# Two normalised tiles turned by DMA instead of TensorE, all residual statistics on VectorE, and one attention split a slot later, in a one-core transformer block

## Chip, cores and metric

The kernel runs on one core of a Trainium2 chip. The metric is device time in microseconds of one execution of the whole program. A core has five engines with a queue each, all in order: TensorE (PE in the profile; PEld is its weight load), VectorE (DVE), ScalarE (ACT), GpSimd (POOL) and SyncE (SP), which here issues nearly all DMAs. An instruction waits on semaphores, and everything queued behind it on its engine waits with it.

## What is computed

One block on 2048 rows of 512 values: layer norm, attention with 32 heads of 16 in which each row sees itself and 7 earlier rows at distance 2, a product with `wo` and a residual sum; then layer norm, a product with `w1` (512 x 1792), squared ReLU, a product with `w2`, and a second residual sum.

```python
h  = x + attention(layernorm(x) @ wqkv) @ wo      # 8 keys per row, 2 apart, softmax
r  = max(layernorm(h) @ w1 + b1, 0)
h2 = h + (r * r) @ w2 + b2
```

All is in float32. The kernel splits each operand of a product in a high and a low part and sums three products of parts (high x high, low x high, high x low), so a product of a 128-row tile costs 12 matmuls of 128 x 512.

## The kernel before

The 2048 rows are 16 tiles t of 128. A first phase makes q, k and v of all tiles; then come four MLP stages, u = 0 to 3, each for the four tiles 4u to 4u + 3 together. While stage u runs its MLP, the attention and the `wo` product of the four tiles of stage u + 1 are done beside it. So tiles 4 to 7 are prepared in stage 0, 8 to 11 in stage 1, 12 to 15 in stage 2; i = t mod 4 is a tile's place in its stage (R = 4, RI = 2).

A stage is a loop over slots p = 0 to 16. Slot p gives TensorE, in this order, a `wo` product if one is due, the first MLP product of hidden block p (`mlp1`, up to p = 13) and the second of block p - 3 (`mlp2`), 12 matmuls each. The order of the instructions of all other engines is the order in which the program writes them, and that is planned by hand: functions are put in lists for a slot, and `end_slot` runs them: first `due` (put there by `at`), then `pump`, then `amid` (by `midway`), then `late` (by `after`). A function that is put in the list being run goes to that list's end.

`pump` draws steps of the attention of the next tiles from a generator. It keeps two clocks in estimated microseconds, `now["pe"]` and `now["dve"]`, and writes steps as long as `dve` is behind `pe`; when `dve` has come to within HALF = 2.6 of `pe` it first runs `amid`. Products add to `pe` (2.73 each), a tile's transposes add 0.44, `norm_stats` adds 0.93 to `dve`, the h add 0.7, `lo_T` of an attention tile 0.69, an attention step 0.26 to 1.55 times a factor of 1.05 to 1.08. The products that weigh the values (L351, VectorE) are summed by three adds on GpSimd (`add_up`, L408), which `pump` writes one step later; the last add writes a head group's part of `o`. An attention unit s serves the two tiles 2s and 2s + 1, in eight head groups.

The way of tile t in slots, with the lists of constants that set them: `load_h` (LH), the split of `o` in two 16-bit planes on ScalarE (`o_split`, L621), a transposing DMA on SP's queue (`turn_dma`, L625), the join of the planes on ScalarE (`o_join`, by `turn_join`, L630) with the casts to high and low part (tiles in OV; OP sets the slots), the `wo` product (WP), `h_add` on VectorE (L666), the statistics of h, the normalisation `h_norm` on ScalarE (L196), `add_b2` on GpSimd (L679) and `spill` of h to DRAM by SP (L682). The normalised tile `hn` must be turned too: for tiles in HV by split, DMA and join (`h_split`, `turn_dma`, `turn_join`, then the casts in `h_parts`), for the others by four transposes on TensorE into a PSUM bank (`h_T`, L201) with the casts read from there. For tiles with i = 2 and 3 of stages 0 and 1 `h_T` stands in slot 16, the last of the stage: the first ahead of the last `mlp2`, the second in its middle. The first product of the next stage reads the casts of all four tiles.

The statistics are made in two ways. Tiles in AS use `act_stats`: two long activations on ScalarE with a short one between (L182 to L184), written in `late`. The others use `norm_stats`: `bn_stats` and `bn_aggr` on VectorE (L163, L164). Either way three small GpSimd instructions, `finish` (L169 to L172, or L188 to L191), make the scale and the offset; `finish` is put in `late`.

SBUF tiles of the name "row" share ROWS = 15 buffers; the products and the transposes for the MLP stages take turns in two PSUM banks.

Of the kernel before, what the change touches and what calls it, by code (L numbers as in the profile page):

```python
# [19 lines left out]
R = 4  # L20
RI = 2
# [8 lines left out]
ROWS = 15  # L30
LAG = 3
HALF = 2.6
AS = (8, 9, 12, 13)
OV = tuple(range(4, 16))
HV = (0,1,4,5,8,9,12,13)
SLOW = 1.01, 1.08, 1.05
DELAY = 3
WJ = 2
# [8 lines left out]
WP = 9, 10, 13, 14  # L47
HP = 15, 15, 16, 16
# [10 lines left out]
def block_kernel(ctx, tc, x, wqkv, wo, w1, b1, w2, b2, out):  # L59
# [53 lines left out]
    def at(delta, fn, *a):  # L113
        due.setdefault(now["slot"] + delta, []).append((fn, a))

    def after(delta, fn, *a):
        late.setdefault(now["slot"] + delta, []).append((fn, a))
# [4 lines left out]
    def end_slot(pe):  # L122
        now["pe"] += pe
        run(due)
        pump()
        run(amid)
        run(late)
        now["slot"] += 1

    def run(chores):  # L130
        todo = chores.get(now["slot"], [])
        while todo:
            fn, a = todo.pop(0)
            fn(*a)

    def dve(t):
        now["dve"] += t
# [18 lines left out]

    stats = {}

    def norm_stats(key, src):
        st = small.tile([P, 6], F32, name="st")  # L160
        mv = small.tile([P, 2], F32, name="mv", bufs=4)
        rs = small.tile([P, 2], F32, name="rs", bufs=4)
        nc.vector.bn_stats(st, src)  # L163
        nc.vector.bn_aggr(mv, st)  # L164
        dve(0.93)
        stats[key] = mv, rs

        def finish():
            nc.gpsimd.tensor_scalar(out=rs[:, 1:2], in0=mv[:, 1:2], scalar1=EPS, scalar2=None,  # L169
                                    op0=ALU.add)  # L170
            nc.gpsimd.tensor_tensor(out=rs[:, 0:1], in0=rs[:, 1:2], in1=mhalf, op=ALU.pow)
            nc.gpsimd.tensor_scalar(out=rs[:, 1:2], in0=mv[:, 0:1], scalar1=rs[:, 0:1],  # L172
                                    scalar2=-1.0, op0=ALU.mult, op1=ALU.mult)
        after(0, finish)

    def act_stats(key, src):

# [263 lines left out]
    def x_stats(t):  # L441
        if t < XS:
            norm_stats(t, xt[t])
        else:
            act_stats(t, xt[t])
# [151 lines left out]
    def o_T(t):  # L597
        s, j = divmod(t, RI)
        pump(until=s)
        tr = transposes(o_t[s][:, j, :])  # L600
        if t % R == RI:

            ohl = att.tile([P, 2, KB, P], F32R, name="ohl", tag="o", bufs=3)
            oT[t] = ohl[:, 0], ohl[:, 1]
        else:
            oT[t] = row("oh", (P, KB, P), F32R), row("ol", (P, KB, P), F32R)
        at(0, hi_T, tr, [oT[t][0]])
        at(0, lo_T, tr, [oT[t][0]], [oT[t][1]])
# [55 lines left out]
    def h_add(t, ps):  # L664
        h = hs[t]
        nc.vector.tensor_tensor(out=h, in0=ps, in1=h, op=ALU.add)  # L666
        dve(0.7)
        if t in AS:
            after(0, act_stats, t, h)
        else:  # L670
            norm_stats(t, h)

    def h_norm(t):
        hn[t] = row("hn")
# [27 lines left out]
    def h_T(t):  # L702
        if t // R == R - 1:
            return last_h_T(t)
        tr = transposes(hn.pop(t), "mm")
        i = t % R
        hs_, ls_ = [a[:, :, i] for a in hh], [a[:, :, i] for a in hl]
        if len(turn["mm"].tags) > 2:
            at(0, hi_T, tr, hs_)
        else:  # L710
            due.setdefault(now["slot"], []).insert(0, (hi_T, (tr, hs_)))
        at(0, lo_T, tr, hs_, ls_)
# [169 lines left out]
    def mlp1(u, f):  # L882
        ps = turn["mm"].tile("mm")
        fs = slice(f * P, (f + 1) * P)
        mm3(ps, lambda k: w1_h[:, k, fs], lambda k: w1_l[:, k, fs],
            lambda k: hh[k // 2][:, k % 2], lambda k: hl[k // 2][:, k % 2])
        at(1, hidden, u, f, ps)
# [94 lines left out]
    for n in range(16):  # L982
        gp, t = divmod(n, 4)
# [28 lines left out]
    def first_phase(t0):  # L1012
        def chores(m):
# [16 lines left out]
            for t in range(R):  # L1030
                if k == OT[t]:
                    at(0, load_h, t)
                    o_T(t)
                if t in HV and k == HK[t][0]:
                    at(0, h_split, t)
                    after(0, turn_dma, ("h", t))
                if t in HV and k == HK[t][1]:
                    at(0, turn_join, ("h", t))
# [3 lines left out]
                if k == HT[t]:  # L1042
                    (at(0, h_parts, t) if t in HV else h_T(t))
            if k in W2:
# [11 lines left out]
    def load_w2(f):  # L1056
        raws[f] = row("raw2")
        nc.sync.dma_start(raws[f], w2[f * P:(f + 1) * P, :])
# [36 lines left out]
    for u in range(R - 1):  # L1095
        now["sub"] = u
        first, end = u == 0, False
        fs = list(range(FB)) if first else [*sorted(place), 12, 13]
        fs += [f for f in range(12) if f not in fs and (u < 2 or f not in ENDS)]
        fs += ENDS if u == 2 else []  # L1100
        need = [] if first else [f for f in fs if f < 12 and f not in place]
        acc = [psum.tile([P, D], F32, name="acc", tag=tag) for tag in ("acc0", "acc1", "tr0", "tr1")]
        js = range(R)


        todo, halves = {}, {}
        for i in js:
            t = R * (u + 1) + i
            if not end:
                a = i // 2 if u == 2 else 0  # L1110
                o0 = OP[i] - a - (2 if i >= RI and t in OV else 0)
                if t in OV:
                    turned = [(o0, after if i == RI else at, 0, o_split, t),
                              (o0, at if i > RI else after, i // (RI + 1), turn_dma, ("o", t)),
                              (o0 + 2, at, 0, o_join, t)]
                else:
                    turned = [(o0, o_T, t)]
                if t in HV:
                    h0 = 11 + i
                    turned += [(h0, midway, 0, h_split, t), (h0, after, 0, turn_dma, ("h", t)),  # L1120
                               (h0 + 2, at, 0, turn_join, ("h", t))]
                for p, *what in ((LH[i] - a, at, 0, load_h, t), *turned,
                                 (WP[i] - a, wo_product, t, (0, 1, 2 + 3 * a, 3 + 3 * a))):
                    todo.setdefault(p, []).append(what)
                p, h = (HP[i], i % 2) if u < 2 else HL[i]
                if t in HV:
                    todo.setdefault(p, []).append((at, 0, h_parts, t))
                else:
                    (todo, halves)[h].setdefault(p, []).append((h_T, t))
            todo.setdefault(UP[i], []).append((at, 0, unspill, R * u + i))  # L1130
        if u == 2:
            for p, *what in ((12, at, 0, t_load, 0), (12, at, 0, t_load, 1), (13, after, 0, t_sums, 0),
                             (13, after, 0, t_sums, 1), (13, at, 1, t_split, 0),
                             (14, after, 0, t_split, 1)):
                todo.setdefault(p, []).append(what)

        def half(p):
            run(due)
            for fn, *a in halves[p]:
                fn(*a)  # L1140

        for p in range(FB + LAG):
            more = 0.0
            if p == FB:
                run(due)
                dve(HOLD)
            if u < 2 and p == FB - 2:
                dve(HOLD)
            for fn, *a in sorted(todo.get(p, []), key=lambda x: x[0] is wo_product):
                fn(*a)  # L1150
                more += 2.73 if fn is wo_product else 0.0
            if p < FB:
                mlp1(u, fs[p])
                more += 2.73
                if first:
                    after(0, split_w2, p)
                    if p + 1 < FB:
                        load_w2(p + 1)
            q = p - LAG
            if q >= 0:  # L1160
                f = fs[q]
                mlp2(u, f, acc, js, q == 0, q == FB - 1,
                     (lambda: half(p)) if p in halves else None)
                more += 2.74
                if f < 12 and (need or first and p < FB - LAG):
                    free.append(place.pop(f))
                    if need:
                        at(1, fetch, need.pop(0))
            end_slot(more)
        for i in js:  # L1170
            at(u // 2, finish, R * u + i, acc[i])
# [48 lines left out]
    h = hs[S // P - 1]  # L1220
# [34 lines left out]
```

## Time and profile before

| what | us |
|---|---|
| median of 3 runs | 506.21 (505.8 to 506.57) |
| the profiled execution | 506.32 |
| its span, first to last instruction | 504.2 |
| TensorE busy | 497.7 (99%) |
| VectorE busy | 377.4 (75%) |
| GpSimd busy | 355.7 (71%) |
| ScalarE busy | 305.0 (60%) |

The granted TensorE clock is 1.000 over the span. In the trace stage 1 begins with the first product at 249.1 and stage 2 at 338.6. In the rows of the timeline the columns are start, length, engine, line, operation, out<-in, shapes, count, and in brackets the engine's idle time before the instruction with what ended it.

### The profile page before, as it was taken

What the parts mean: (1) busy time and instruction counts of PE and PEld (TensorE: products, weight loads), DVE (VectorE), ACT (ScalarE), POOL (GpSimd) and SP (SyncE); (2) the same over time, 40 slices, a digit from 0 to 9 for tenths busy, and PEclk for the clock granted to TensorE, in tenths of its full rate; (3) what the DMA queues carried; (4) which work ended last, traced back from release to release, by engine and by line L of the source; (5) the groups of instructions that cost most, each with busy time, mean ns of one, the idle gap of its engine ahead of it and who ended that gap; (6) DMA issues with size and microseconds to landing.
All of it is one profiled execution on the core that took longest, in us unless ns stands there. A gap on an engine that the chain in (4) does not pass through costs nothing.

```text
span 504.2 us, 7546 instructions
## 1 busy us (share of the span) xinstructions
PE 497.7 (99%) x2422; PEld 421.4 (84%) x2422; DVE 377.4 (75%) x512; ACT 305.0 (60%) x558; POOL 355.7 (71%) x434
## 2 busy tenths in 40 slices
PE   8999999999999999999999999999999999999997
PEld 7999888888888888888888888778888888998986
DVE  6379899988989899788879988998972047833233
ACT  4635777668346758378464657845566937666541
POOL 5614798886685999879677876896897464685610
PEclk9999999999999999999999999999999999999999
DMA  9668979989798898679577766767662372355212
GB/s 273 196 209 229 311 231 311 281 261 278 211 230 249 300 282 255 212 209 231 186 255 219 211 194 167 208 229 257 204 174 67 97 197 83 132 153 154 64 43 83
DMA packets 109359, 102.61 MB, mean 204 GB/s; under 512 B 29448, under 2 KB 77832, under 8 KB 109320
## 3 DMA queue, kind: packets, MB, share of 16 engines
q1 hardware_dynamic: 108376, 101.61, 68.4%
q10 hardware_dynamic: 944, 0.52, 0.3%
q8 instruction: 19, 0.31, 0.2%
q14 instruction: 20, 0.16, 0.1%
HBM read 72.65 MB, written 24.25 MB: 192 GB/s over the span
## 4 chain that ended last, share of the span: by engine, by line
PE 88%; ACT 4%; POOL 3%; DVE 2%; issue 1%; DMA 1%; POOLq 0%; ACTq 0%
PE mm L228 46%; PE acc L900 25%; PE wo L228 8%; PE mm L823 6%; PE tr L201 2%; POOL pr L408 1%; DMA xt<-in_A_x_dram 1%; ACT pl L621 1%; DVE pr L351 0%; ACT pl L630 0%; ACT big_l L152 0%; ACT r L877 0%; ACT r L876 0%; DVE s L759 0%; PE half L923 0%
## 5 line engine op out<-in xcount | busy, mean ns | idle before, releaser
L408 POOL TENSOR_TENSOR pr<-pr 128x512 f32<-128x512 f32 (+1 forms) x128 | 134.1, 1048 | 33.6 <-DVE pr L351 28.2
L228 PE MATMUL mm<-big_l,w_h 128*128 128x512 f32 x336 | 88.5, 389 | 0.1
L351 DVE TENSOR_TENSOR pr<-ex,v 128x1024 f32<-128x1024 f32 x64 | 78.0, 1220 | 12.2 <-POOL o L408 7.5
L340 DVE TENSOR_TENSOR pr<-qp,k 128x1024 f32<-128x1024 f32 x64 | 76.8, 1200 | 10.1 <-ACT qp L268 7.8
L374 DVE TENSOR_REDUCE ex<-pr 128x64 f32<-128x1024 f32 x64 | 78.5, 1226 | 1.9
L228 PEld LDWEIGHTS mm<-big_l,w_h 128*128 128x128 f32 x336 | 63.0, 188 | 13.6 <-ACT qp L268 0.5
L155 POOL TENSOR_TENSOR rl<-r,rh 128x512 fp32r<-128x512 f32 x42 | 55.4, 1319 | 20.2 <-ACT rh L152 20.2
L228 PE MATMUL mm<-big_l,xh 128*128 128x512 f32 (+1 forms) x208 | 55.8, 378 | 0.0
L228 PE MATMUL mm<-big_h,xh 128*128 128x512 f32 (+1 forms) x208 | 53.7, 379 | 0.7 <-ACT xh L152 0.7
L228 PE MATMUL mm<-big_h,xl 128*128 128x512 f32 (+1 forms) x208 | 52.7, 375 | 0.0
L900 PE MATMUL acc<-big_l,rh 128*128 128x512 f32 x190 | 52.2, 390 | 0.0
L900 PE MATMUL acc<-big_h,rh 128*128 128x512 f32 x190 | 52.1, 391 | 0.0
L900 PE MATMUL acc<-big_h,rl 128*128 128x512 f32 x190 | 51.7, 389 | 0.0
L228 PE MATMUL mm<-big_l,w_l 128*128 128x512 f32 x168 | 44.9, 389 | 0.0
L228 PEld LDWEIGHTS mm<-big_h,xh 128*128 128x128 f32 x208 | 37.7, 188 | 7.6 <-ACT xh L152 1.9
L228 PEld LDWEIGHTS mm<-big_h,xl 128*128 128x128 f32 x208 | 38.2, 188 | 6.3 <-DVE xl L155 0.5
L900 PEld LDWEIGHTS acc<-big_h,rl 128*128 128x128 f32 x190 | 35.7, 188 | 7.4
L900 PEld LDWEIGHTS acc<-big_l,rh 128*128 128x128 f32 x190 | 35.5, 188 | 7.4
L228 PEld LDWEIGHTS mm<-big_l,xh 128*128 128x128 f32 x208 | 37.5, 188 | 4.9
L876 ACT ACTIVATE r<-mm,b_sb 128x512 f32<-128x512 f32 x42 | 28.7, 684 | 19.9 <-PE mm L228 19.8
L900 PEld LDWEIGHTS acc<-big_h,rh 128*128 128x128 f32 x190 | 34.9, 188 | 6.7
L528 ACT COPY y<-mm 128x512 f32<-128x512 f32 x36 | 21.1, 585 | 26.4 <-PE mm L228 23.5
(167 smaller groups left out, 924.9 us busy)
## 6 DMA issues: line engine op xcount, KB each, us to landing
k<-qkv_d SPq DMA_DIRECT2D x48, 288.0 KB, 3.4
v<-qkv_d SPq DMA_DIRECT2D x48, 288.0 KB, 3.6
qkv_d<-y SPq DMA_DIRECT2D x18, 512.0 KB, 4.1
big_l<-w2l_d SPq DMA_DIRECT2D x24, 256.0 KB, 2.6
xt<-in_A_x_dram SPq DMA_DIRECT2D x16, 256.0 KB, 4.3
q<-qkv_d SPq DMA_DIRECT2D x32, 128.0 KB, 3.4
h<-in_A_x_dram SPq DMA_DIRECT2D x16, 256.0 KB, 3.6
h_d<-h SPq DMA_DIRECT2D x16, 256.0 KB, 3.0
```

The costliest lines, as they stand in the source:

```text
L155: eng.tensor_tensor(out=dst, in0=src, in1=h, op=ALU.subtract)
L201: nc.tensor.transpose(tr[:, k, :], src[:, k * P:(k + 1) * P], ident)
L228: nc.tensor.matmul(ps, l(k), r(k), start=(n == 0), stop=(n == 3 * KB - 1))
L340: nc.vector.tensor_tensor(out=pr.rearrange("p i w h d -> p i w (h d)"), in0=qps["now"][:, j % 2].unsqueeze(2).to_broadcast([P, RI, W, GC]) ...
L351: nc.vector.tensor_tensor(out=p2, in1=vwin, op=ALU.mult, in0=e1[:, :, :, j * GH:(j + 1) * GH].unsqueeze(4).to_broadcast([P, RI, W, GH, DH]))
L374: nc.vector.tensor_reduce(out=lf[:, :, :, j * GH:(j + 1) * GH], in_=pr, axis=X, op=ALU.add)
L408: nc.gpsimd.tensor_tensor(out=dst, in0=p2[:, :, :w], in1=p2[:, :, w:2 * w], op=ALU.add)
L528: nc.scalar.copy(dst, src)
L621: nc.scalar.copy(two_planes(planes[key][1]), halves_of(src))
L823: nc.tensor.matmul(ps, sta[y][:, k], mov[x][:, k], start=(first and q == 0), stop=(last and q == len(terms) - 1), skip_group_check=True)
L876: nc.scalar.activation(r, ps, AF.Relu, bias=b1_sb[:, f:f + 1])
L900: nc.tensor.matmul(acc[j], l[:, j * P:(j + 1) * P], w[f], start=(first and n < len(js)), stop=(last and n >= len(terms) - len(js)))
```

## The change

Tiles 6 and 10 join HV: their normalised tile is split, turned by DMA and joined. The split and the DMA are written in `late` of the slot of the `wo` product (13), and `h_norm` of these tiles moves one slot forward to stand before them; the join and `h_parts` are put in `due` of slot 16. AS becomes empty, so that tiles 8, 9, 12 and 13 use `norm_stats`. For tiles 4 to 13 `finish` goes in `due`, ahead of the slot's `pump`, instead of `late`. In stage 2 the `o_split` of tile 14 moves from `late` of slot 9 to `due` of slot 10, and its DMA from `late` of slot 9 to `late` of slot 10.

```diff
-AS = (8, 9, 12, 13)
+AS = ()
 OV = tuple(range(4, 16))
-HV = (0,1,4,5,8,9,12,13)
+HV = (0,1,4,5,6,8,9,10,12,13)
...
-    def norm_stats(key, src):
+    def norm_stats(key, src, soon=False):
...
-        after(0, finish)
+        (at if soon else after)(0, finish)
...
-            norm_stats(t, h)
+            norm_stats(t, h, R <= t < 14)
...
-                    turned = [(o0, after if i == RI else at, 0, o_split, t),
-                              (o0, at if i > RI else after, i // (RI + 1), turn_dma, ("o", t)),
+                    turned = [(o0 + a * (i == RI), after if i == RI and not a else at, 0, o_split, t),
+                              (o0 + a * (i == RI), at if i > RI else after, i // (RI + 1), turn_dma, ("o", t)),
                               (o0 + 2, at, 0, o_join, t)]
...
-                if t in HV:
+                if t in HV and i == RI:
+                    turned += [(WP[i], at, 0, after, 0, h_split, t),
+                               (WP[i], at, 0, after, 0, turn_dma, ("h", t)),
+                               (HP[i], at, 0, turn_join, ("h", t))]
+                elif t in HV:
...
-                                 (WP[i] - a, wo_product, t, (0, 1, 2 + 3 * a, 3 + 3 * a))):
+                                 (WP[i] - a, wo_product, t,
+                           (0, int(i != RI or t not in HV), 2 + 3 * a, 3 + 3 * a))):
```

Here a is 1 for tiles 14 and 15 and 0 for the others, and the four numbers given to `wo_product` are the slots, counted from its own, of `h_add`, `h_norm`, `add_b2` and `spill`.

## The prediction

> **What bounds the kernel now.** The page first: who is busy over the span.
>
> ```profile
> span 504.2 us, 7546 instructions
> ...
> PE 497.7 (99%) x2422; PEld 421.4 (84%) x2422; DVE 377.4 (75%) x512; ACT 305.0 (60%) x558; POOL 355.7 (71%) x434
> ```
>
> TensorE is occupied to 99%, so an edit pays only by taking instructions or waits from TensorE, and costs only by making TensorE wait. Next the chain of waits in order of time (start, length, what) at the ends of MLP stages 0 and 1 and at tile 10's wo product, the places in the touched stages where it isn't plain matmuls in a row.
>
> ```profile
> 239.95 5.44 PE acc L900 x24
> 245.39 0.44 PE tr L201 x4
> ```
>
> A 128x512 matmul takes 5.44 / 24 = 0.227 us of TensorE; the four transposes of tile 6 take 0.44, and tile 10's are the same instructions. For the wo product of tile 10 the timeline shows what TensorE waited for and what filled ScalarE until then.
>
> ```profile
> 306.87 1.05 ACT L621 COPY pl<-o 128x1024 uint16<-128x1024 uint16 x1 [2.10 <-POOL o L408]
> 307.83 0.63 ACT L182 ACTIVATE scrap<-h 128x512 f32<-128x512 f32 x1
> 309.53 0.67 ACT L876 ACTIVATE r<-mm,b_sb 128x512 f32<-128x512 f32 x1
> ...
> 316.25 1.07 PE L900 MATMUL acc<-big_h,rl 128*128 128x512 f32 x4
> 317.44 0.62 ACT L152 CAST ohl<-pl 128x512 fp32r<-128x512 f32 x1
> 318.11 1.19 PE L228 MATMUL wo<-wo_h,ohl 128*128 128x512 f32 x4 [0.79 <-ACT ohl L152]
> ```
>
> TensorE could have gone on at 316.25 + 4 x 0.227 = 317.16; it started at 318.11, 0.95 late. ScalarE had work without a gap from 306.87, when GpSimd delivered `o`: tile 10's split, from 307.83 to 309.53 the statistics of tile 9 (1.70), then queued work up to `ohl`, done at 318.06.
>
> **The change part by part.** The profiled execution took 506.32 us (span 504.2, 2.1 around it), 0.11 above the median 506.21; I sum against the first and take the difference off at the end.
>
> *Transposes of tiles 6 and 10.* Off TensorE: 2 x 0.44 = 0.88, if nothing then waits. In their place each tile gets a split on ScalarE, a DMA on SP's queue and a join on ScalarE, priced by the lines of the tiles turned now (the split by the 1.05 of `pl` above, the same copy; the join in ns, least, median, most; the DMAs of the same kind from issue to landing):
>
> ```profile
> L630 ACT COPY pl<-hn x8: 1155/1172/1177, 152.5 to 418.5; 128x1024 uint16<-128x1024 uint16 x8
> ```
>
> ```profile
> DMA to landing us min/median/max: 3.6/3.7/5.2
> ```
>
> So 1.05 + 3.7 + 1.17 = 5.9 us (to 7.4 with the slowest landing) where TensorE needed 0.44. Whether that is hidden depends on when it may start. The Trainium skill ("VectorE: DVE Perf Modes", section Rules for kernel authors) says to transpose 128x128 on TensorE if the result may lie in PSUM, and by DMA otherwise, and it speaks against this edit. By that rule the edit loses, and its own part of my sum agrees (1.1 at stage 0, less 0.44 and 0.2 at stage 1, is +0.5); by TensorE's rows alone it would be -0.88.
>
> *Rstd issued at once, in stage 0.* `finish` (three GpSimd instructions) now stands ahead of the attention adds of its slot instead of behind them. In slot 10 the adds of the last head group for tile 6 fall behind tile 5's `finish`, which needs `mv`.
>
> ```profile
> 213.51 0.70 DVE L163 BATCH_NORM_STATS2 st<-h 128x6 f32<-128x512 f32 x1
> 214.24 0.18 DVE L164 BATCH_NORM_AGGREGATE mv<-st 128x2 f32<-128x6 f32 x1
> 215.34 2.12 POOL L408 TENSOR_TENSOR pr<-pr 128x512 f32<-128x512 f32 x2
> 218.04 1.05 ACT L621 COPY pl<-o 128x1024 uint16<-128x1024 uint16 x1 [1.72 <-POOL o L408]
> 218.09 0.23 POOL L169 TENSOR_SCALAR rs<-mv 128x1 f32<-128x1 f32 x1
> 219.07 0.27 POOL L172 TENSOR_SCALAR rs<-mv,rs 128x1 f32<-128x1 f32 x1
> ...
> 227.94 0.62 ACT L152 CAST ohl<-pl 128x512 fp32r<-128x512 f32 x1
> 228.68 0.87 PEld L228 LDWEIGHTS wo<-wo_h,ohl 128*128 128x128 f32 x4
> ```
>
> `finish` takes 219.34 - 218.09 = 1.25. It cannot start before 214.5, so the adds start at 215.7, not 215.34: 0.4 later. ScalarE goes from `pl` to `ohl` (228.56) without a gap, and TensorE's weight load follows 0.1 behind. Tile 6's wo product then waits about 0.2, which the wait below swallows. From slot 11 GpSimd has hardly a gap up to the end of the stage, so its later work shifts by 0.4 too.
>
> *End of stage 0.* The new join of tile 6 stands in ScalarE's queue behind the normalisation of tile 7 and ahead of tile 7's casts; the DMA stands in SP's queue behind the spill of tile 5, which waits for `add_b2` of tile 5 on GpSimd.
>
> ```profile
> 241.00 1.29 POOL L679 TENSOR_TENSOR h<-h,b_sb 128x512 f32<-128x512 f32 x1
> 242.32 0.32 SPq L682 DMA_DIRECT2D h_d<-h  x1
> ...
> 246.39 0.82 ACT L196 ACTIVATE hn<-h,rs 128x512 f32<-128x512 f32 x1 [0.71 <-POOL rs L172]
> 247.11 0.62 ACT L152 CAST big_l<-tr 128x256 fp32r<-128x256 f32 x2
> 247.26 0.66 PE L201 MATMUL tr<-ident,hn 128*128 128x128 f32 x4
> ...
> 249.14 1.09 PE L228 MATMUL mm<-big_l,w_h 128*128 128x512 f32 x4
> ```
>
> Tile 6's `finish`, behind that `add_b2` until now, moves ahead of it. The `add_b2` (241.00) therefore ends 1.25 + 0.4 later than 242.29, at 243.9. The spill follows, then the DMA at 244.3; it lands at 248.0 (249.5 at worst). The join runs to 249.2, tile 6's two casts to 249.8, the first cast of tile 7 (0.31) to 250.15. The first product of stage 1 needs that cast and starts at 250.2 instead of 249.14: +1.1. Tile 6's 0.44 is lost here: TensorE waited at 247.26 for `hn` of tile 7 before, and without tile 6's transposes it only comes to that wait earlier. Bounds: 0 if DMA and join were done before `hn` of tile 7 and that came as before; +2.6 with a landing of 5.2.
>
> *Statistics of tiles 8 and 9 on VectorE, stage 1.* ScalarE loses 1.70 a tile. VectorE gets `bn_stats` and `bn_aggr`, 0.92 a tile (213.51 to 214.42 above). GpSimd gets `finish` of tile 9 ahead of slot 10's adds.
>
> ```profile
> 298.76 2.49 POOL L408 TENSOR_TENSOR pr<-pr 128x512 f32<-128x512 f32 x2 [1.34 <-DVE pr L351]
> 301.04 0.69 DVE L666 TENSOR_TENSOR h<-wo,h 128x512 f32<-128x512 f32 x1 [0.61 <-PE wo L228]
> 301.33 0.46 POOL L408 TENSOR_TENSOR o<-pr 128x128 f32<-128x128 f32 x1
> ...
> 304.17 2.13 POOL L408 TENSOR_TENSOR pr<-pr 128x512 f32<-128x512 f32 x2
> ```
>
> The adds at 298.76 were written by the fifth step that `pump` took in slot 9. Its budget, worked through in the code's own costs: `dve` is 282.15 at the slot's start, in both kernels. Before, four steps, the h add and `lo_T` brought it to 288.7, short of `pe` at 289.83, so a fifth step ran. Now the statistics add 0.93 and `pe` is 0.44 lower (tile 6's transposes): 289.68 against 289.39, and the fifth step moves to slot 10, behind tile 9's `finish`. That `finish` waits for the wo product: h add 301.04, `mv` at 302.7, done at 304.0. Both groups of adds then queue: 304.0 to 306.7 and to 309.4 (2.7 each, as 304.17 to 306.85). So `o` comes 2.5 later than 306.85, ScalarE's queue is 1.70 shorter, and `ohl` is ready 0.8 to 1.1 later than 318.06: TensorE loses about 1.0 more. Bounds: if the fifth step stayed in slot 9, `o` would be only 0.9 late, and 0.8 of the 0.95 wait would go; adds of 3.0 instead of 2.7 (298.76 to 301.79 is that) twice would make it +1.6.
>
> *End of stage 1.* TensorE saves 0.44, and the 0.3 that it lost between the last product and the next stage's first (337.38 + 4 x 0.227 = 338.29), which I read as waiting for the PSUM bank of tile 10's transposes:
>
> ```profile
> 337.38 1.09 PE L900 MATMUL acc<-big_h,rl 128*128 128x512 f32 x4
> 338.59 1.15 PE L228 MATMUL mm<-big_l,w_h 128*128 128x512 f32 x4
> ```
>
> The join (1.17) and two casts (0.62) of tile 10 now stand between `hn` of tile 11 and its casts, as in stage 0, with GpSimd's queue about as late as TensorE's. I give back 0.1 to 0.2 for that (an estimate: it would be nothing with `hn` 1 us earlier, and 1.1 as in stage 0). Net -0.6.
>
> *Nothing for the rest.* Tiles 12 and 13: attention is over, nothing urgent queues behind their `finish`. Tile 14's split: its wo product reads `ohl`, which has cover.
>
> ```profile
> 397.03 0.69 DVE L155 TENSOR_TENSOR ohl<-pl,ohl 128x512 fp32r<-128x512 f32 x1 [5.79 <-ACT ohl L152]
> 401.22 1.07 PE L228 MATMUL wo<-wo_h,ohl 128*128 128x512 f32 x4
> ```
>
> The low part is done at 397.72, 3.5 before TensorE asks for the high one at 401.22. The split now stands behind the three activations of slot 10 (about 2: 0.67 for the first, above), its DMA behind the fetch and the load of that slot; the join follows a slot later, as before behind that slot's activations, so it moves by less. Cost 0; without the cover, whatever it came late.
>
> The sum: +1.1 (stage 0) + 1.0 - 0.6 = +1.5 on 506.32, or 507.7 on the runs' scale.
>
> **The rivals.** *ScalarE's relief decides* (faster). Where the fifth step's adds stay ahead of `finish`, the wait at tile 10 shrinks by 0.8, tile 10's transposes go and the bank's wait with them: -0.8 - 0.44 - 0.3 = -1.5, and with stage 0 at its lower bound of 0 that is 504.7. For it: ScalarE's gapless 11.2 us ahead of the wait hold 1.70 of statistics. Against: the order in which GpSimd's queue is written. It decides as soon as `o` of tile 10 is less than 1.70 late.
>
> *The two ends cancel* (no change): stage 0 costs its 1.1, stage 1 gains about as much, or GpSimd's wait comes but the DMA of tile 6 does not: 506.2.
>
> *The landing decides* (slower still): the slowest landing of 5.2 at both ends: 1.5 more at stage 0 and up to 1 at stage 1: about 509.5. Nothing says that it is usual; 3.7 is the median.
>
> **How the numbers follow.** Forecast 0.48, relief 0.25, cancelling 0.17, landing 0.10. A measurement of this kernel can tell about 0.2%, 1.0 us, from no change, so the edges are 505.2 and 507.2. The forecast's own range is 506.7 to 508.6; about 0.38 of it lies above the edge, 0.10 below. Slower: 0.38 + 0.10 + 0.03 from the third case = 0.51. Faster: 0.23 of the relief. The rest, 0.26, is the same. The range takes in the relief's middle and the forecast with a late landing: 504.8 to 509.0.
>
> **What would show it.** Right: eight fewer transposes of `hn`; a gap of 2 to 3 us on GpSimd at tile 9's `finish` with adds behind it; TensorE's wait at tile 10's wo product near 1.9; the first product of stage 1 waiting for a cast behind a join. Wrong: that wait near 0.2, or the join of tile 6 done before `hn` of tile 7.

## The result, and the profile after

| | before | after |
|---|---|---|
| median of 20 runs, us | 506.46 (505.67 to 508.02) | 507.60 (506.58 to 509.85) |
| profiled execution, us | 506.32 | 508.40 |
| its span, us | 504.2 | 506.6 |

The ratio of after to before is 1.0022, 95% interval 1.0013 to 1.0032: slower, by 1.14 us in the medians. The first profile of after is one of its slower executions, so its pieces add up to more than the medians differ. A second profile of the same kernel (experiment 9) is used beside it. By its interval the difference is clear of the noise, and it is small: a fifth of a per cent.

The profile page of after, its span and busy times:

```profile
span 506.6 us, 7521 instructions
...
PE 497.4 (98%) x2414; PEld 420.4 (83%) x2414; DVE 381.3 (75%) x520; ACT 302.1 (60%) x542; POOL 356.1 (70%) x434
```

TensorE has eight transposes fewer and is still the bound; its share fell by a point, which is waiting. The timeline of TensorE in after shows where (start, length, engine, line, operation; the bracket is the idle time and what ended it):

```profile
227.98 1.07 PE L900 MATMUL acc<-big_h,rl 128*128 128x512 f32 x4
229.90 1.19 PE L228 MATMUL wo<-wo_h,ohl 128*128 128x512 f32 x4 [0.85 <-ACT ohl L152]
...
246.35 1.52 PE L900 MATMUL acc<-w_x,rh 128*128 128x512 f32 x6
248.74 0.66 PE L201 MATMUL tr<-ident,hn 128*128 128x128 f32 x4 [0.87 <-ACT hn L196]
...
250.81 1.20 PE L228 MATMUL mm<-big_l,w_h 128*128 128x512 f32 x4
...
318.04 1.07 PE L900 MATMUL acc<-big_h,rl 128*128 128x512 f32 x4
320.58 1.20 PE L228 MATMUL wo<-wo_h,ohl 128*128 128x512 f32 x4 [1.47 <-ACT ohl L152]
...
337.94 0.61 PE L900 MATMUL acc<-big_l,rh 128*128 128x512 f32 x2
339.03 0.66 PE L201 MATMUL tr<-ident,hn 128*128 128x128 f32 x4 [0.48 <-ACT hn L196]
...
341.10 1.19 PE L228 MATMUL mm<-big_l,w_h 128*128 128x512 f32 x4
```

The same places in the kernel before, where the wo product of tile 10 and the transposes of tile 7 (247.26) stand in the rows of the prediction:

```profile
228.00 1.07 PE L900 MATMUL acc<-big_h,rl 128*128 128x512 f32 x4
228.90 1.07 PE L228 MATMUL wo<-wo_h,ohl 128*128 128x512 f32 x4
...
336.02 0.62 PE L900 MATMUL acc<-big_l,rh 128*128 128x512 f32 x2
336.48 0.60 PE L201 MATMUL tr<-ident,hn 128*128 128x128 f32 x4
```

With 0.227 us a matmul the waits in after are 1.01 at the wo product of tile 6 (229.90; none before), 1.03 at the transposes of tile 7 (248.74; 0.21 before, counted from the start of the last matmul ahead of them), 1.63 at the wo product of tile 10 (320.58; 0.95 before) and 0.64 at the transposes of tile 11 (339.03; none before). All four end with ScalarE's output.

The stages of every profiled kernel, from the first product of one stage to that of the next, in us (read off TensorE's timelines), and the waits at the two wo products. The first product of stage 0 falls between 160.5 and 162.2 in these executions although the first phase's code is the same in all, so kernels are compared stage by stage, not by their spans.

| kernel | stage 0 | wo(6) wait | stage 1 | wo(10) wait | stage 2 to end |
|---|---|---|---|---|---|
| before | 88.24 | 0.0 | 89.45 | 0.95 | 165.61 |
| after, first profile | 89.93 | 1.01 | 90.29 | 1.63 | 165.50 |
| after, second profile (9) | 89.05 | 0.1 | 90.34 | 1.66 | 165.51 |
| 1 after, finish late | 88.72 | 0.0 | 88.90 | 0.20 | 165.53 |
| 2 before, finish early | 88.87 | 0.1 | 89.72 | 0.93 | 165.61 |
| 3 before, AS empty | 88.25 | 0.0 | 88.52 | 0.39 | 165.51 |
| 4 before, DMA turn | 88.66 | 0.0 | 89.58 | 0.95 | 166.61 |
| 5 after, finish(4) late | 89.99 | 1.05 | 90.31 | 1.64 | 165.58 |
| 6 after, no DMA turn | 88.85 | 0.1 | 88.73 | 0.55 | 165.52 |
| 7 kernel 1, late add_b2 | 87.53 | 0.0 | 88.74 | 0.21 | 165.50 |
| 8 kernel 3, late add_b2 | 88.00 | 0.0 | 88.54 | 0.40 | 165.43 |
| 10 kernel 7, finish(11) early | 87.53 | 0.0 | 87.97 | 0.21 | 166.89 |
| 11 before, tile 14 | 88.22 | 0.0 | 89.40 | 0.93 | 165.66 |

From stage 2 on, after is as before: everything happens in stages 0 and 1. (The 166.61 of kernel 4 and the 166.89 of kernel 10 hold a wait of 1.05 and 1.20 shortly after stage 2 begins; both are explained below.)

### The profile page after: what moved, and what is told of

Its sections match the earlier page's. It is cut to its first block, busy times and chain, and to the rows that moved or that the text cites. A ratio compares the mean times of both kernels' runs of the same rounds, so it can differ in the third digit from the quotient of the medians.

```text
span 506.6 us, 7521 instructions
## 1 busy us (share of the span) xinstructions
PE 497.4 (98%) x2414; PEld 420.4 (83%) x2414; DVE 381.3 (75%) x520; ACT 302.1 (60%) x542; POOL 356.1 (70%) x434
## 4 chain that ended last, share of the span: by engine, by line
PE 38%; POOL 5%; ACT 4%; DVE 3%; issue 2%; DMA 0%; SPq 0%; POOLq 0%; ACTq 0%; DVEq 0%
PE acc L900 16%; PE mm L228 12%; PE mm L823 6%; PE wo L228 3%; POOL pr L408 1%; POOL rl L155 1%; ACT hn L196 1%; POOL h L679 1%; ACT pl L621 1%; ACT r L877 1%; ACT r L876 1%; DVE pr L351 0%; POOL rs L171 0%; DMA q<-qkv_d 0%; ACT big_l L152 0%
## 5 line engine op out<-in xcount | busy, mean ns | idle before, releaser
L351 DVE TENSOR_TENSOR pr<-ex,v 128x1024 f32<-128x1024 f32 x64 | 78.1, 1222 | 12.1 <-POOL o L408 8.8
L340 DVE TENSOR_TENSOR pr<-qp,k 128x1024 f32<-128x1024 f32 x64 | 76.9, 1202 | 10.4 <-ACT qp L268 8.5
L228 PEld LDWEIGHTS mm<-big_l,w_l 128*128 128x128 f32 x168 | 31.5, 188 | 6.6
```

The source lines that it names most:

```text
L228: nc.tensor.matmul(ps, l(k), r(k), start=(n == 0), stop=(n == 3 * KB - 1))
L340: nc.vector.tensor_tensor(out=pr.rearrange("p i w h d -> p i w (h d)"), in0=qps["now"][:, j % 2].unsqueeze(2).to_broadcast([P, RI, W, GC]) ...
L351: nc.vector.tensor_tensor(out=p2, in1=vwin, op=ALU.mult, in0=e1[:, :, :, j * GH:(j + 1) * GH].unsqueeze(4).to_broadcast([P, RI, W, GH, DH]))
```

## The experiments

The theory at the start: the order on GpSimd costs the time, because `finish` now stands ahead of attention adds. The rivals: A, the DMA turn of tiles 6 and 10; B, the statistics on VectorE. Times are medians; each ratio is to the kernel before, run on the same chip, with its 95% interval.

### 1 to 4: the change taken apart

**1, after with `finish` late but for tiles 6 and 10.**

```diff
-            norm_stats(t, h, R <= t < 14)
+            norm_stats(t, h, t in (6, 10))
```

> The changed kernel, with finish back in late for all tiles but 6 and 10 (which need it early, because their h_norm was moved forward). Theory (the order on GpSimd costs): the adds for tile 6 no longer stand behind finish(5), so wo(6) loses its wait of 1.0 to 1.1 us, GpSimd is 1.3 us earlier up to the end of stage 0, and the first product of stage 1 comes near 249.6 instead of 250.81; in stage 1 the first of the two groups of adds starts at about 302 (its product ends at 301.99) instead of 305.75, so o(10) comes 1.3 to 1.5 us earlier and the wait at wo(10) falls from 1.64 to 0.2 to 0.5. Together 2.3 to 2.6 us less than the changed kernel: 505.0 to 505.4, faster than the kernel before by about 1. Rival A (the DMA turn of tile 6, its join ahead of tile 7's casts, is the cost): no more than 0.3 less than the changed kernel, 507.3. Rival B (the statistics on VectorE and the step of the pump that they move are the cost): wo(6) gains its 1.1, the wait at wo(10) stays near 1.6: 506.5.

506.22 against 506.16, ratio 1.0002 (0.9993 to 1.0011): 1.4 below the median of after, or 1.1 when each is counted from the kernel before of its own set, and not 2.4. Both wo products came out as the theory said (no wait, and 0.20), but the waits before the transposes of tiles 7 and 11 stayed, 0.96 and 0.68. Without the early finish the net loss is gone; but the statistics on VectorE bring 0.9 alone (experiment 3), and that gain is not to be seen here, so something else still costs as much.

**2, before with the early finish alone.** As in the diff of the change: `soon`, with `R <= t < 14`.

> The kernel before with the early finish alone (tiles 4, 5, 6, 7, 10 and 11; tiles 8, 9, 12, 13 keep the statistics on ScalarE). Theory: the adds of slot 10 of stage 0 start 1.25 to 1.3 us later behind finish(5), wo(6) waits about 1.1; GpSimd stays 1.3 late but so is TensorE, and the 0.2 that TensorE waited for hn(7) goes: +0.9 to +1.1 in all, 507.4 to 507.6. Rival A (the DMA turn is the cost): GpSimd makes the 0.4 of the prediction, which is swallowed, 506.5. Rival C (finish ahead of add_b2 and of the last adds pays): faster, 506.0.

507.52, ratio 1.0025 (1.0015 to 1.0036). The total is the theory's, the place is not: wo(6) waited 0.10 and not 1.1. TensorE waited 0.59 for `hn` of tile 7, and 0.62 at the start of stage 2 for a low cast on VectorE.

**3, before with AS empty alone.**

```diff
-AS = (8, 9, 12, 13)
+AS = ()
```

> The kernel before with AS empty alone: tiles 8, 9, 12 and 13 by norm_stats, finish in late. Theory: in slot 9 of stage 1 the planner's clocks are 289.68 against 289.83, so the fifth step stays in slot 9, its adds stay ahead of finish(9), o(10) is at most 0.3 late and ScalarE's queue 1.70 shorter: the wait at wo(10) falls from 0.95 to 0.1 to 0.3, total -0.7 to -0.9, 505.6 to 505.8. Rival B (statistics on VectorE delay the attention by themselves): o(10) comes 1 or more late, wait of 0.9 or more, 506.4 to 507.

505.26, ratio 0.9982 (0.9972 to 0.9991): faster, more than foretold. The wait at wo(10) is 0.39, and the 0.30 before stage 2 is gone as well. Rival B is out: this part of the change pays about 0.9.

**4, before with the DMA turn of tiles 6 and 10 alone** (HV, the new split, DMA and join, `h_norm` one slot earlier; `finish` early for these two tiles, which the moved `h_norm` needs).

> The kernel before with tiles 6 and 10 turned by DMA alone, with the early finish for these two tiles only, as their moved h_norm needs. Theory: the join of tile 6 still stands between hn(7) and tile 7's casts, but hn(7) is 1.3 earlier than in the changed kernel; first product of stage 1 near 249.5, +0.4; end of stage 1 -0.3 to +0.2; wait at wo(10) unchanged near 0.95 (the fifth step stays, 288.7 against 289.39): 506.4 to 507.0, no difference that counts. Rival A (the DMA turn is the cost): +1.1 at stage 0 and nothing back, 507.6. Rival D (TensorE's 0.88 of transposes is really saved): 505.6.

508.01, ratio 1.0033 (1.0021 to 1.0045), outside the theory's range. Stage 0 is +0.42 as expected and wo(10) waits 0.95 as expected; rival A's 1.1 in stage 0 is not there. What was not expected is VectorE, whose low parts come late (timeline of VectorE, then of GpSimd, in this kernel):

```profile
336.28 6.19 DVE L155 TENSOR_TENSOR big_l<-pl,big_l 128x256 fp32r<-128x256 f32 x6
```

```profile
336.45 2.27 POOL L408 TENSOR_TENSOR pr<-pr 128x512 f32<-128x512 f32 x2 [1.21 <-DVE pr L351]
338.80 0.53 POOL L408 TENSOR_TENSOR o<-pr 128x128 f32<-128x128 f32 x1
339.29 2.90 POOL L679 TENSOR_TENSOR h<-h,b_sb 128x512 f32<-128x512 f32 x2
```

Six casts that take 0.4 us each elsewhere need 6.19 while GpSimd works without a pause from 336.45 to 342.19. The product of stage 2 that reads them waited 1.05, and wo(11) had waited 0.72 in the same way.

### 5, 6 and 9: why wo(6) waited in one profile and not in the other

In slot 7 of stage 0, `ol` of tile 4 on VectorE and `rl` on GpSimd start within 0.5 us of each other in 11 of the 13 profiles (1.0 and 1.1 apart in experiments 6 and 4). Before (VectorE, then GpSimd):

```profile
200.05 0.67 DVE L155 TENSOR_TENSOR ol<-pl,oh 128x512 fp32r<-128x512 f32 x1
```

```profile
200.09 1.80 POOL L155 TENSOR_TENSOR rl<-r,rh 128x512 fp32r<-128x512 f32 x1
```

After, first profile:

```profile
200.35 1.70 DVE L155 TENSOR_TENSOR ol<-pl,oh 128x512 fp32r<-128x512 f32 x1
```

```profile
200.21 1.29 POOL L155 TENSOR_TENSOR rl<-r,rh 128x512 fp32r<-128x512 f32 x1
...
203.26 1.29 POOL L408 TENSOR_TENSOR pr<-pr 128x512 f32<-128x512 f32 x1 [1.76 <-DVE pr L351]
```

Whichever starts first takes its own time (0.67 or 1.29), and the other is held until it ends: `rl` lasts 1.80 instead of 1.29, or `ol` lasts 1.70 and ends 0.55 after `rl`. Where GpSimd is first, the product behind `ol` is late, and GpSimd waits 1.76 for it: its adds start at 203.26 instead of 201.93. The Trainium skill ("SBUF — State Buffer", section "SBUF: two separate sides") says that VectorE, where an instruction has two SBUF inputs, and GpSimd share a pair of ports that the first to start keeps for its whole instruction; these rows agree. Not every VectorE instruction is held up so. Its attention products (L340 and L351), which have one input in PSUM, take 1.16 to 1.23 us in the kernel before, whether or not GpSimd adds beside them.

The theory for 5: the pause of 1.49 ahead of the adds of slot 8 used to take such a delay up, and the early `finish` of tile 4 now fills it.

**5, after with `finish` of tile 4 late.**

```diff
-            norm_stats(t, h, R <= t < 14)
+            norm_stats(t, h, 5 <= t < 14)
```

> The changed kernel with finish back in late for tile 4 alone. Theory (two causes meet: in slot 7 of stage 0 the low part ol of tile 4 on VectorE and rl on GpSimd hold each other up, and where GpSimd starts first its queue is 1.28 us later; the pause before the adds of slot 8, 1.49 in the kernel before, used to take that up, and finish(4) now fills the pause): with finish(4) behind them the adds of slot 8 start within 0.3 us of where they did before (47.7 us after the stage's first product), the adds of slot 10 at 54.8 after it instead of 55.75, and wo(6) waits at most 0.2 instead of 1.0, whichever engine starts first. 0.5 to 0.9 us less than the changed kernel, 506.8 to 507.1. Rival E (finish(5) alone makes wo(6) late): the wait stays near 1.0, 507.6.

508.55, ratio 1.0035 (1.0020 to 1.0050). Half of the theory held: the adds of slot 8 started 47.7 after the stage's first product again. The other half fell: those of slot 10 started at 55.79, and wo(6) waited 1.05 although `ol` was first here. With `finish(4)` late its 1.25 us stand ahead of the adds of slot 10 again, and `finish(5)` adds another 1.25. So the early `finish(4)` makes room for `finish(5)` by running in a pause; in the first profile of after the delay from the ports took that room away.

**6, after without the DMA turn.**

```diff
-HV = (0,1,4,5,6,8,9,10,12,13)
+HV = (0,1,4,5,8,9,12,13)
```

> The changed kernel with tiles 6 and 10 back on TensorE (early finish and AS empty stay). Theory: stage 0 costs what the early finish costs, +0.6 (wo(6) in time) to +1.3 (wo(6) 1.0 late); in slot 9 of stage 1 pe is 0.44 higher again, the fifth step stays there, the adds behind finish(9) start at 304.0 to 304.2 on the scale of the kernel before, and the wait at wo(10) falls to 0.2 to 0.5; the 0.30 before stage 2 stays or goes. Sum -0.3 to +0.4 against the kernel before, 505.9 to 506.6, so 1.0 to 1.7 below the changed kernel. Rival F (the early finish(9) by itself holds the adds): wait at wo(10) stays near 1.6, 507.0 to 507.6.

505.61, ratio 0.9988 (0.9973 to 1.0003), a little below the expected range. wo(10) waits 0.55, against the 0.2 to 0.5 expected: the fifth step is back in slot 9 (its adds start at 301.49, ahead of the h add at 302.58), so an early `finish(9)` alone does not hold `o` up. So the DMA turn takes part at wo(10), through the 0.44 that it takes off the planner's clock. With it (after) the wait is 1.6; with it and a late `finish(9)` (experiment 1) 0.20.

**9, after once more.**

> The changed kernel once more, unchanged, for a second profile. Theory (the 1.0 at wo(6) in its first profile came from which engine went first in slot 7 of stage 0): if VectorE's ol (L155) starts ahead of GpSimd's rl this time and takes about 0.7, the adds of slot 10 start 54.8 us after the stage's first product instead of 55.75, wo(6) waits 0.1 to 0.2, stage 0 takes 88.9 to 89.3 instead of 89.93 and the execution about 507.4; if rl is first again, all is as in the first profile. Stage 1 as before near 90.3 either way. Rival E (finish(5) makes wo(6) late in any case): wo(6) waits 1.0 with ol first, too.

508.20, ratio 1.0034 (1.0017 to 1.0051). `ol` was first this time (0.68 us; `rl` 1.80). GpSimd in slot 10 of stage 0, second profile and then first:

```profile
214.07 1.30 POOL L155 TENSOR_TENSOR rl<-r,rh 128x512 fp32r<-128x512 f32 x1
215.81 0.23 POOL L169 TENSOR_SCALAR rs<-mv 128x1 f32<-128x1 f32 x1 [0.44 <-DVE mv L164]
...
217.01 2.12 POOL L408 TENSOR_TENSOR pr<-pr 128x512 f32<-128x512 f32 x2
```

```profile
214.06 1.28 POOL L155 TENSOR_TENSOR rl<-r,rh 128x512 fp32r<-128x512 f32 x1
215.43 0.23 POOL L169 TENSOR_SCALAR rs<-mv 128x1 f32<-128x1 f32 x1
...
216.63 2.12 POOL L408 TENSOR_TENSOR pr<-pr 128x512 f32<-128x512 f32 x2
```

The stage began at 162.20 and at 160.88. In the second profile `finish(5)` waits 0.44 for `mv`, and the adds start 54.81 after the stage's first product; in the first they start at 55.75, with no wait ahead of `finish(5)`, since `rl` ended only then. Before it was 54.44. wo(6) waited 0.1 and stage 0 took 89.05, as the theory of the ports said; rival E is out for this execution.

### 7, 8 and 10: what the DMA turn needs

In kernel 1 TensorE waits for `hn` of tiles 7 and 11. `finish(7)` stands behind `add_b2` of tile 5 on GpSimd, so that was moved.

**7, kernel 1 with `add_b2` and `spill` of tiles 5 and 9 two slots later.**

```diff
-                           (0, int(i != RI or t not in HV), 2 + 3 * a, 3 + 3 * a))):
+                           (0, int(i != RI or t not in HV), 2 + 3 * a + 2 * (i == 1 and u < 2),
+                            3 + 3 * a + 2 * (i == 1 and u < 2)))):
```

> The first of these experiments (changed kernel, early finish for 6 and 10 alone), with add_b2 and spill of tiles 5 and 9 two slots later, so behind finish(7) and finish(11) on GpSimd and behind the transposing DMA of tiles 6 and 10 on SP. Theory (hn of tile 7 and 11 is what TensorE waits for, and it is late because add_b2 of 1.29 us stands ahead of its finish): hn comes 1.2 to 1.3 us earlier, the waits of 0.96 and 0.68 before the transposes of tiles 7 and 11 go, and the DMA lands by 244.5, so the join is done well before the casts: -1.6 to -2.0 on that kernel, 504.2 to 504.7. Rival A (the join between hn(7) and its casts is what costs): the waits only move to the first product of the next stage, 505.5 to 506.2. Rival G (the later spills are paid for at the stage's start, by row buffers or by what SP then holds up): no gain or a loss, 506.2 or more.

504.63, ratio 0.9969 (0.9957 to 0.9981), in the theory's range; with experiment 10 it is the fastest of these kernels. TensorE at the end of stage 0, then ScalarE, in this kernel:

```profile
244.87 1.52 PE L900 MATMUL acc<-w_x,rh 128*128 128x512 f32 x6
246.23 0.60 PE L201 MATMUL tr<-ident,hn 128*128 128x128 f32 x4
```

```profile
244.90 0.82 ACT L196 ACTIVATE hn<-h,rs 128x512 f32<-128x512 f32 x1 [1.33 <-POOL rs L172]
245.62 1.15 ACT L630 COPY pl<-hn 128x1024 uint16<-128x1024 uint16 x1
246.81 0.71 ACT L152 CAST big_l<-pl 128x256 fp32r<-128x256 f32 x2
```

`hn` is done at 245.72, ahead of the transposes, and the join still stands between it and the casts without costing anything. Stage 0 gained 1.19 on kernel 1. Stage 1 gained only 0.16: the wait of 0.66 for `hn` of tile 11 stayed.

**8, kernel 3 with the same move** (no DMA turn).

> The kernel before with AS empty, with add_b2 and spill of tiles 5 and 9 two slots later; all finishes in late, tiles 6 and 10 on TensorE. Theory: the 0.33 before the transposes of tile 7 goes and nothing else changes, 504.9 to 505.1. If this kernel is above the other with late add_b2, the DMA turn of tiles 6 and 10 pays once hn of tiles 7 and 11 is early, by up to 0.8. Rival G (the later spills cost at the stage's start): 505.3 or more.

505.81, ratio 0.9994 (0.9980 to 1.0008); stage 0 took 0.25 less than in kernel 3, as expected, but the median did not show it. By stages the DMA turn (7 against 8) brings 0.47 in stage 0 and costs 0.20 in stage 1. The medians of 7 and 8 lie 1.18 apart, but from stage 0 to the end their profiles differ by 0.20 only; in the profile of 8 the first phase ended 0.90 later (161.43 against 160.53). So the medians alone don't show what the turn is worth here.

**10, kernel 7 with `finish(11)` ahead of the last block's `rl` in stage 1.**

```diff
-        (at if soon else after)(0, finish)
+        finish() if key == 11 else (at if soon else after)(0, finish)
...
-        at(0, lo, nc.vector if u == R - 1 else nc.gpsimd, rl, r, rh)
+        (after if u == 1 and f == fs[-1] else at)(0, lo, nc.vector if u == R - 1 else nc.gpsimd, rl, r, rh)
```

> The kernel with late add_b2 that turns tiles 6 and 10 by DMA, with finish(11) written ahead of the last block's rl on GpSimd instead of behind it (stage 1 alone). Theory: in that kernel GpSimd waits from 328.5 to 330.9 for rh with mv(11) ready at 329.3, so finish(11) ends near 330.7 instead of 333.8, hn(11) starts when tile 9's casts end, 0.8 earlier, and the 0.66 before the transposes of tile 11 goes; up to 0.2 of it comes back at the first product of stage 2, behind the casts. -0.4 to -0.7, 503.9 to 504.3. Rival H (the join of tile 10 and the casts set the first product of stage 2, not hn): no change, 504.6.

505.25, ratio 0.9971 (0.9957 to 0.9985), the same as kernel 7. The 0.66 went and came back 3 us later. TensorE, VectorE and GpSimd in this kernel:

```profile
339.76 0.50 PE L228 MATMUL mm<-big_l,w_h 128*128 128x512 f32 x1 [1.03 <-DVE big_l L155]
```

```profile
332.88 4.70 DVE L155 TENSOR_TENSOR big_l<-pl,big_l 128x256 fp32r<-128x256 f32 x4 [1.03 <-ACT big_l L152]
```

```profile
332.79 4.16 POOL L679 TENSOR_TENSOR h<-h,b_sb 128x512 f32<-128x512 f32 x3
```

GpSimd's three adds of b2 now start 0.09 before VectorE's low casts of tiles 8 and 9, which need 4.70 instead of the 1.43 that they took in after. The low casts of tiles 10 and 11 come later for it, and TensorE waits 1.20. Neither the theory nor rival H foresaw this.

### 11: tile 14

```diff
-                    turned = [(o0, after if i == RI else at, 0, o_split, t),
-                              (o0, at if i > RI else after, i // (RI + 1), turn_dma, ("o", t)),
+                    turned = [(o0 + a * (i == RI), after if i == RI and not a else at, 0, o_split, t),
+                              (o0 + a * (i == RI), at if i > RI else after, i // (RI + 1), turn_dma, ("o", t)),
```

> The kernel before with the later split of tile 14 alone. Theory: the low part of tile 14 has 3.5 us of cover, so nothing changes: 506.0 to 506.5, stage 2 to the end 165.4 to 165.7 as before. Rival: the split behind the three activations holds up the join, and wo(14) waits: over 506.8.

506.39 against 506.26, ratio 0.9999 (0.9986 to 1.0013); stage 2 to the end takes 165.66. It costs nothing.

## Why the prediction was right, and where it was off

The forecast, 507.7 with +1.5 over before, is what the runs show (507.60; in the second set 508.20 against 506.26). Its mechanism at wo(10) is the one in the trace. In the second profile the three terms are +0.8, +0.7 and +0.2, where +1.1, +1.0 and -0.6 were forecast. Two terms were 0.3 too large each and one was 0.8 too small, so that the errors nearly cancelled: that the total came out so well is in part luck. One effect, the ports, was not seen at all.

**Tile 10's wo product: right in kind, 0.3 too large.** The fifth step moved to slot 10, and both groups of adds queue behind `finish(9)`. GpSimd, then ScalarE, in the first profile of after:

```profile
304.55 0.23 POOL L169 TENSOR_SCALAR rs<-mv 128x1 f32<-128x1 f32 x1 [2.57 <-DVE mv L164]
...
305.75 2.11 POOL L408 TENSOR_TENSOR pr<-pr 128x512 f32<-128x512 f32 x2
307.94 0.47 POOL L408 TENSOR_TENSOR o<-pr 128x128 f32<-128x128 f32 x1
308.37 2.11 POOL L408 TENSOR_TENSOR pr<-pr 128x512 f32<-128x512 f32 x2
```

```profile
311.05 1.05 ACT L621 COPY pl<-o 128x1024 uint16<-128x1024 uint16 x1 [2.29 <-POOL o L408]
...
319.91 0.62 ACT L152 CAST ohl<-pl 128x512 fp32r<-128x512 f32 x1
```

Less the 1.67 by which stage 1 began later, `o` arrives at 309.4, the forecast's 309.4. From the split to `ohl` ScalarE takes 8.86 instead of 10.57, which is the 1.70 of the statistics. `ohl` ends at 318.86 on that scale, 0.8 later than 318.06: the lower end of the 0.8 to 1.1 that the prediction worked out, of which it carried 1.0. TensorE loses 0.68 more, not 1.0: it came to this product 0.12 later in the stage, so that much of the 0.8 is no wait. Experiments 1 and 6 show that it takes the moved step and the early `finish(9)` together.

**Stage 0: +1.1 forecast, +0.8 and +1.7 found.** The order was as predicted: `add_b2(5)`, spill, DMA; `hn(7)`, join, casts of 6, cast of 7, first product. The term that the second profile bears out is the 0.4 of slot 10 (0.37 there; 0.39 in experiment 2), with a wait of 0.1 at wo(6). The first profile shows what the prediction left out: where GpSimd wins the ports in slot 7, the whole 1.25 of `finish` counts, and wo(6) waits 1.01. The prediction took `mv` for the only bound on `finish(5)`; the other is `rl`, just ahead of it on GpSimd. Counted from the stage's first product, `mv` is there at 53.52 in both profiles, and `rl` ends at 53.17 in the second and 54.46 in the first. The end of the stage was late for another reason than the prediction's chain of DMA, join and cast: the join waits for `hn(7)` and not for the DMA. In the second profile the transposes of tile 7 begin 0.62 later in the stage than before: the 0.37 of slot 10, and `rl` ahead of `finish(7)`, which takes 1.48 instead of 1.29 beside VectorE's low casts, are most of it. TensorE had come to them 0.44 earlier for nothing. At the first product of stage 1 it waits another 0.19, for a cast behind the join; only this is the step that the prediction named. Experiment 7, with the join in the same place and `hn` early, loses nothing there. Its move also let the DMA start 3.9 earlier in the stage than in kernel 1, so that run doesn't tell the two apart.

**End of stage 1: -0.6 forecast, +0.2 found.** This is the step that failed. The prediction gave back 0.1 to 0.2 for the join and called it an estimate; the profiles show 0.64 at the transposes of tile 11 and 0.20 at the first product of stage 2. ScalarE and GpSimd in after say why:

```profile
338.16 0.81 ACT L196 ACTIVATE hn<-h,rs 128x512 f32<-128x512 f32 x1 [0.71 <-POOL rs L172]
338.88 1.15 ACT L630 COPY pl<-hn 128x1024 uint16<-128x1024 uint16 x1
```

```profile
335.23 1.30 POOL L155 TENSOR_TENSOR rl<-r,rh 128x512 fp32r<-128x512 f32 x1 [1.22 <-ACT rh L152]
336.61 0.46 POOL L169 TENSOR_SCALAR rs<-mv 128x1 f32<-128x1 f32 x1
```

`finish(11)` stands behind `rl` of the last block, which waits for `rh`, and on ScalarE `rh` now stands behind `hn` and the split of tile 10. This `rh` ends 82.8 after the stage's first product in kernel 7 and 80.6 in kernel 3, which has no DMA turn. Taking `finish(11)` out from behind that `rl` removed the wait (experiment 10). The prediction priced the join's place on ScalarE and not the split's. Its reading of the 0.3 lost before stage 2, as a wait for the bank of tile 10's transposes, fits the rows: in the kernel before TensorE's weight load starts 0.12 after VectorE's second low cast from that bank ends, and in experiment 3, where that cast ends 0.58 ahead of the load, there is no wait.

**Nothing for tile 14, and for tiles 12 and 13**: right (experiment 11; stage 2 to the end 165.61 and 165.50).

**The rivals.** ScalarE's relief alone does bring a faster kernel, 505.26 (experiment 3, -0.9), where the rival said -1.5; in this change it is eaten by the order of the adds and by the DMA turn. By the medians against the kernel before, the statistics bring 0.9 (experiment 3), the DMA turn takes 1.0 of it back (experiment 1), and the early `finish` costs the remaining 1.1. These shares hold for this order of taking the change apart, since at wo(10) the DMA turn and the early `finish` cost together what neither costs alone. The landing never decided: the join of tile 6 starts right behind `hn(7)` in both profiles of after and in kernels 1, 4 and 7. In after that is 3.15 after the DMA's issue, sooner than the 3.6 that the prediction had as the shortest landing. The rule of the Trainium skill that the prediction quoted ("VectorE: DVE Perf Modes", section "Rules for kernel authors", transposes into PSUM on TensorE) held in this change, where the DMA turn costs about 1 (experiment 1 against 3). With `hn` early it turns round in stage 0, -0.47 by one profile each of 7 and 8.

**Open.** How often GpSimd wins in slot 7 of stage 0: in 4 of the 13 profiles here it started first (after's first, and experiments 1, 3 and 11), and of these only after paid for it at wo(6). The medians of after lie 1.14 and 1.94 above before, its two profiles' stages 2.4 and 1.6; which share of the executions lost the 0.9 was not measured. The stages are read from one profile of each kernel, two of after, and the medians hold the first phase too; whether its length differs between these kernels in the mean was not measured.

## What to carry to other kernels

On an in-order engine, a small instruction that is moved ahead costs its whole length to everything behind it unless it lands in a pause, and a pause that it fills is no longer there to take up the next delay. Taking work off the bounding engine pays only where the next input is ready: make the input early first (here three small instructions ahead of one long add), then take the transposes away. Where a planner keeps clocks, work its decisions through again with the new costs: 0.44 us moved a step across a `finish` here.

## What the runs showed of the hardware that was not expected

VectorE's subtractions with two SBUF inputs and GpSimd's adds and subtractions hold each other up whole, and a lead of 0.04 to 0.14 us at the start decides which waits: `ol` takes 0.67 or 1.70, `rl` 1.29 or 1.80, and at the worst six casts took 6.19 us. Products with one input in PSUM (L340, L351) were not held up. This gate lay behind the 1.05 of experiment 4 and the 1.20 of experiment 10, and through GpSimd's lateness behind the 1.01 at wo(6) in the first profile. The other surprise is the first phase: with the same code it ended anywhere from 160.5 to 162.2 us, a spread as large as the whole effect studied here; the two profiles of after alone lie 1.32 apart.
